# A fixed order for the score matmuls and DFT shares of one cycle

## The chip, the cores and the metric

The kernel runs on one core of one Trainium2 chip. The metric is the device time of the kernel in microseconds (us); three runs of the kernel before gave a median of 2001.87 us (2001.1 to 2004.49).

## The reference

The output is a gated mix of two blocks over x (2048 rows, 640 features, float32):

```python
g = sigmoid((x * gate_w).sum(-1, keepdims=True))
a = mha(x, wqkv, wo)          # 32 heads of 20: softmax(q k^T / sqrt(20)) v, then @ wo
b = dft_seq_re @ (x @ dft_hid_re.T) - dft_seq_im @ (x @ dft_hid_im.T)
return g * a + (1 - g) * b
```

`wqkv` and `wo` are scaled by 64, so scores are large and the softmax needs the true row maximum.

## The kernel before, in words

A first part (the page's slices up to about 280 us) projects q, k and v, stores them to DRAM scratch and starts the hidden DFT. After the loop described next, a last part (from about 1922 us) multiplies by `wo`, gates and stores.

The **main loop** does everything else together. The heads go in pairs; one head of a pair lies on partitions 0 to 63 of `kst` and `qst`, the other on 64 to 127, so that a matmul on one head uses one row half of TensorE. A unit `n` is a head pair and half of the 2048 queries; a unit has 32 steps `i`, and a step has two scores of each of two kinds, one for each head `h`:

- **e** (L636 in `mixed`): keys by queries with the row maximum already in two extra rows of `q`, read by ScalarE's exponential (L639) into a probability tile `p`.
- **m** (L151 in `s_mm`): queries by keys, 41 steps (`LEAD`) ahead, read by VectorE's maximum (L153) into `mx`. It serves only to get the row maxima of a later unit.

Each of the two takes the next of five PSUM banks in turn (`bank()`, `ps`); a bank comes free when its reader has ended. Every score takes its bank in the order in which the program issues it, so each waits for the reader of the score five earlier.

Between the scores stand the **shares** of the DFT (`fill`): each `next(fills)` issues two matmuls of 320 columns, one on each row half, into the two banks `yp` (L287 in the hidden DFT, L509 in the sequence DFT). A hidden tile has 15 shares, a unit of the sequence DFT 48; at the end of either, ScalarE and VectorE read the two banks (L295 and L296, L528 and L529), put on a list by the share and issued at the next burst by `run_extras`. POOL prepares the operands of the sequence DFT.

Every fourth step ends a **cycle** with the **burst**: `av_step` twice, 16 matmuls of the probabilities of the four steps past with the values (L434). They use all 128 rows, four columns' groups at once.

When a unit's maxima are complete, `s_end` negates and joins them (L159, `nms`), and two steps later calls `max_chain`: a transpose on TensorE (L179, it takes a bank too), a cast and a subtract on VectorE (L94 and L95, `m`), and two steps later four small DMAs on SP's queue into the two extra rows of `q`.

The order of work is written out by hand: the program's order is each engine's order. In the kernel before, a step is: e of head 0, m of head 1, shares, e of head 1, m of head 0, shares (in the fourth step of a cycle the burst instead). So a cycle has seven places for shares. `goals` says how many shares are to be done by each place; it deals out 15 for each of the first 54 cycles, and 48 over three or four cycles for each of the 56 units of the sequence DFT. The transpose, where there is one, comes just before the burst, in the cycle's last step.

Of the kernel before, what the change touches and what calls it, by code (L numbers as in the profile page):

```python
# [12 lines left out]
AF = mybir.ActivationFunctionType  # L13
# [5 lines left out]
P = 128  # L19
# [3 lines left out]
DH = 20  # L23
ND = D // P
NS = S // P
NP = H // 2
HE = D // 2
VW = 2 * (DH + 1)
KROWS = 3 * DH
NU = 2 * NP  # L30
BW = HE + 2
LEAD = 41
HEAD = 10

# [16 lines left out]
def f32(ap):  # L51
    return ap.bitcast(F32)
# [3 lines left out]
def mix_kernel(ctx: ExitStack, tc: tile.TileContext, xa, wqk, wb, cdft, wo, out):  # L56
    nc = tc.nc
    pe, act, dve, pool, sp = nc.tensor, nc.scalar, nc.vector, nc.gpsimd, nc.sync
# [23 lines left out]
    kst = [const.tile([P, S], R, name=f"kst{i}") for i in range(2)]  # L82
# [7 lines left out]
    def split(dst1, dst2, src, e1, e2):  # L90
        if e1 is act:
            act.activation(dst1, src, AF.Copy)  # L92
        else:
            e1.tensor_copy(dst1, src)  # L94
        e2.tensor_tensor(dst2, src, f32(dst1), op=ALU.subtract)  # L95
# [8 lines left out]
    def bank():  # L104
        return ps_w.tile([P, 512], F32, name=f"ps{next(turn) % 5}")

    def pair_tile():
        return work.tile([P, 2, 512], F32, name="p", bufs=5)
# [10 lines left out]
    def load_stack(p):  # L119
        kt, qt = kst[p % 2], qst[p % 2]  # L120
        u = S // 2
        for t, o, two, one, cs in ((kt, D, 0, 2, slice(0, S)), (qt, 0, 1, 0, slice(0, u)), (qt, 0, 1, 0, slice(u, S))):
            for h in range(2):
                r = (2 * p + h) * DH
                b = 64 * h
                rows = slice(o + r, o + r + DH)
                yield f32(t[b + two * DH : b + (two + 2) * DH, cs]), qk_scr[:, rows, cs]
                yield f32(t[b + one * DH : b + (one + 1) * DH, cs]), qk_scr[0, rows, cs]

    def q_unit(n):  # L130
        u = n % 2 * (S // 2)
        return qst[n // 2 % 2][:, u : u + S // 2]

    mx, nms = {}, {}
    now, later = [-1], {}

    def at_step(i, fn):
        later.setdefault(i, []).append(fn)


    def s_mm(i, h):
        n, s = divmod(i, 32)
        if n >= NU:
            return lambda: None
        qt, kc = divmod(s, 4)
        q, k = q_unit(n), kst[(n // 2) % 2]
        if n not in mx:
            mx[n] = small.tile([P, 2, 8, 4], F32, name="mx", bufs=2)
        ps = bank()
        b = 64 * h  # L150
        pe.matmul(ps, q[b : b + KROWS, qt * P : (qt + 1) * P],  # L151
                  k[b : b + KROWS, kc * 512 : (kc + 1) * 512], start=True, stop=True)
        return lambda: dve.tensor_reduce(mx[n][:, h, qt, kc : kc + 1], ps, axis=AX.X, op=ALU.max)  # L153

    def s_end(i):
        n, s = divmod(i, 32)
        if n < NU and s == 31:
            nms[n] = small.tile([P, 16], F32, name="nm", bufs=2)
            dve.tensor_reduce(nms[n], mx.pop(n).rearrange("p h q c -> p (h q) c"), axis=AX.X, op=ALU.max, negate=True)  # L159
        if s == 1 and 0 < n <= NU:  # L160
            max_chain(n - 1)

    def s_step(i):
        for fn in [s_mm(i, h) for h in range(2)]:
# [11 lines left out]
    def max_chain(n):  # L176
        q = q_unit(n)
        pt = bank()[:16, :P]
        pe.transpose(pt, nms.pop(n), ident)  # L179
        m1 = small.tile([16, P], R, name="m1", bufs=2)  # L180
        m2 = small.tile([16, P], R, name="m2", bufs=2)
        split(m1, m2, pt, dve, dve)

        def rows():
            for h in range(2):
                b = 64 * h + KROWS
                sp.dma_start(f32(q[b : b + 1, :]), f32(m1[8 * h : 8 * h + 8, :]))
                sp.dma_start(f32(q[b + 1 : b + 2, :]), f32(m2[8 * h : 8 * h + 8, :]))

        if now[0] < 0:  # L190
            rows()
        else:
            at_step(now[0] + 2, rows)
# [27 lines left out]
    def load_wb(j, e1=act, e2=dve):  # L221
        raws = []
        for d in range(0, ND, 3):
            n = min(3, ND - d)
            raw = raw_tile()[:, : n * BW].rearrange("p (d c) -> p d c", d=n)
            sp.dma_start(raw, wb[j, :, d : d + n])
            raws.append((d, n, raw))

        def finish():
            w = proj.tile([P, 2, ND, BW], R, name="wb", bufs=2)  # L230
            for d, n, raw in raws:
# [7 lines left out]
    def flush(keep=0):  # L239
        while len(stores) > keep:  # L240
            sp.dma_start(*stores.pop(0))
# [118 lines left out]
    for n, c in enumerate(order):  # L360
        for t in range(4):
            m = 4 * n + t
# [4 lines left out]
            if t == 1:  # L367
                fin()
                if n + 2 < len(order):
                    fin = load_wqk(order[n + 2])  # L370
    run_s(LEAD)
    flush()
# [16 lines left out]
    cparts, vts, pts = {}, {}, {}  # L389
# [38 lines left out]
    def av_step(i, n, kt):  # L428
        v = vts[n // 2]
        pp = [pts.pop((n, kt, qc)) for qc in range(2)]  # L430
        for qc in range(2):
            for h in range(2):
                j = 2 * qc + h
                pe.matmul(av[32 * j : 32 * j + DH + 1, :], v[:, kt, h * (DH + 1) : (h + 1) * (DH + 1)],  # L434
                          pp[qc][:, h, :], start=kt == 0, stop=kt == NS - 1)
        if kt == NS - 1:
            unit_end(i, n)
# [110 lines left out]
    def run_extras(g, most):  # L548
        while extras and most and extras[0][0] <= now[0]:
            extras.pop(0)[1]()  # L550
            most -= 1
        if more(g):
            n = g // (HT * NS) + 1
            preps.append(load_a(n, made.setdefault(n, 0)))
            made[n] += 1
        if len(preps) > 2 or preps and not more(g):
            preps.pop(0)()
# [8 lines left out]
    def start_dft():  # L566
        flush()
        proj.release()
        apool.append(pools(name="apool", bufs=1))
# [13 lines left out]
    total = 32 * NU  # L583
    done = 0
    goals, fins = {}, {}
# [4 lines left out]
    HID = 4 * NS - HEAD  # L590
# [4 lines left out]
    start = 4 * HID  # L595
    HIDS = HID * 3 * ND
# [4 lines left out]
    cycles += [(edge[u], edge[u + 1], 3 * NS) for u in range(UNITS)]  # L601
    at_goal = 0
    for c0, c1, count in cycles:
        slots = [(4 * c + k, z) for c in range(c0, c1) for k in (1, 2, 3, 4) for z in range(2 - k // 4)]
        for f, slot in enumerate(slots):
            goals[slot] = at_goal + count * (f + 1) // len(slots)
        at_goal += count

    def fill(i, z):
        nonlocal done  # L610
        while done < goals.get((i, z), 0):
            next(fills)
            done += 1

    for i in range(total + 1):
        now[0] = i
        n, s = divmod(i, 32)
        for fn in later.pop(i, ()):
            fn()
        if s % 2 == 0:  # L620
            flush()
        if i < total:
            kt, qc = divmod(s, 2)
            if s == 0 and n % 2 == 0:
                p = n // 2
                if p + 1 < NP:
                    at_step(i + 6, functools.partial(load_v, p + 1))
                    for j, args in enumerate(load_stack(p + 1)):
                        at_step(i + 2 + 2 * j, functools.partial(pool.dma_start, *args))
            q, k = q_unit(n), kst[(n // 2) % 2]  # L630
            pp = pts[n, kt, qc] = pair_tile()

            def mixed(h):
                b = 64 * h
                pt = bank()
                pe.matmul(pt, k[b : b + KROWS + 2, kt * P : (kt + 1) * P],  # L636
                          q[b : b + KROWS + 2, qc * 512 : (qc + 1) * 512], start=True, stop=True)
                most = s_mm(i + LEAD, 1 - h)
                act.activation(pp[:, h], pt, AF.Exp, scale=float(DH) ** -0.5)  # L639
                most()  # L640

            mixed(0)
            fill(i, 0)
            mixed(1)
            s_end(i + LEAD)
        if start + 2 <= i < start + 2 + HT:
            for k in range(2):
                at_step(i + 3, load_a(0, 2 * (i - start - 2) + k))
        if i and i % 4 == 0:
            run_extras(max(done - HIDS, 0) // 3, 2)  # L650
            j = i // 2 - 2
            for kt in (j, j + 1):
                av_step(i, kt // NS, kt % NS)
        else:
            fill(i, 1)
        if i % 4 == 2:
            c = i // 4
            if c + HEAD in (NS, 2 * NS):
                load_wb(3 + (c + HEAD) // NS, pool, pool)()
            if c in (HID - 5, HID - 3):  # L660
                load_c((c - HID + 5) // 2)()
            if c == HID + 1:
                cfin.append(load_c(2))
        if i == start:
            start_dft()
        if total - 10 <= i < total - 4 and i % 2 == 0:
            tt = (i - total + 10) // 2
            fins[tt] = load_o(tt)
        if i == total - 3:
            fins[0]()  # L670
    assert done == at_goal
    now[0] = total + 4
    run_extras(2 * NS * UNITS, 99)
# [76 lines left out]
```

## Time and profile before

| | |
|---|---|
| median of three runs | 2001.87 us (2001.1 to 2004.49) |
| the profiled execution's own time | 2004.27 us |
| its span, first to last instruction | 2002.5 us |
| mean granted TensorE clock | 0.996 |
| busy: TensorE, VectorE, ScalarE, POOL | 99%, 71%, 63%, 55% of the span |
| maxima (L153) | 2048, mean 682 ns |
| exponentials (L639) | 2048, mean 599 ns |
| e and m scores (L636, L151) | 2048 each |
| matmuls of the sequence DFT (L509) | 5376 |
| matmuls of the bursts (L434) | 4096 |

A row of the timeline gives the start in us from the span's start, the length in us, the engine (PE is TensorE's matmul, PEld its weight load, DVE VectorE, ACT ScalarE), the line, the tiles and how many instructions were merged into the row; in brackets stands the idle time before it and what ended it. A row of a group gives the count, the busy time in us, the mean ns of one, and the idle time before them. A matmul's recorded length begins when it is handed to the array, and includes the wait for its weights.

### The profile page before, as it was taken

The page shows a single profiled execution, that of the slowest core. Times are in us where ns is not written, and L with a number is a line of the kernel's source. Part 1 is how long each engine was busy: PE and PEld are TensorE (multiplying, and loading weights), DVE is VectorE, ACT ScalarE, POOL GpSimd, SP SyncE. Part 2 cuts the span into 40 slices and gives each one's busy share as a digit, 9 for nine tenths or more (in the row PEclk, how much of TensorE's full clock was granted, in tenths as well). Part 3 has the DMA queues.
Part 4 walks back from the last instruction along what each step waited for, and adds up shares of the span by engine and source line. Part 5 has one row for each costly group of instructions (what it writes and reads, how often), then busy time and mean ns, then how long its engine had stood idle before and what let it go on. Part 6 is the DMA issues. An engine that isn't in the chain of part 4 may idle for free. (4 is left out here: it accounts for less than half of the span.)

```text
span 2002.5 us, 44148 instructions
## 1 busy us (share of the span) xinstructions
PE 1972.5 (99%) x17080; PEld 1402.0 (70%) x17080; DVE 1428.3 (71%) x2419; ACT 1253.5 (63%) x2337; POOL 1096.9 (55%) x1010
## 2 busy tenths in 40 slices
PE   8999999999999999999999999999999999999998
PEld 7987767666775666666666666666666666666678
DVE  3144568878887788778877877888778877887323
ACT  4221147767776667667766766677667766676741
POOL 1210001111005999657479888994776789777534
PEclk9999999999999999999999999999999999999999
DMA  7654321312115475435266747563545566453355
GB/s 223 166 169 142 126 80 45 83 50 78 40 52 163 148 212 156 119 110 150 88 169 195 204 138 202 187 188 106 158 145 143 155 176 191 143 165 119 99 152 180
DMA packets 196514, 281.05 MB, mean 140 GB/s; under 512 B 73372, under 2 KB 137916, under 8 KB 194384
## 3 DMA queue, kind: packets, MB, share of 16 engines
q1 hardware_dynamic: 158992, 246.20, 40.2%
q0 software_dynamic: 37312, 32.03, 6.5%
q8 instruction: 134, 2.20, 0.5%
q14 instruction: 76, 0.62, 0.1%
HBM read 213.81 MB, written 63.70 MB: 139 GB/s over the span
## 5 line engine op out<-in xcount | busy, mean ns | idle before, releaser
L153 DVE TENSOR_REDUCE mx<-ps 128x1 f32<-128x512 f32 x2048 | 1263.7, 682 | 294.7 <-PE ps L151 281.3
L639 ACT ACTIVATE p<-ps 128x512 f32<-128x512 f32 x2048 | 1122.5, 599 | 438.8 <-PE ps L151 334.5
L151 PE MATMUL ps<-kst,qst 60*128 60x512 f32 x2048 | 924.2, 459 | 9.2 <-ACT p L639 4.1
L636 PE MATMUL ps<-qst,kst 62*128 62x512 f32 x2048 | 818.9, 407 | 2.1 <-DVE mx L153 0.9
L509 PE MATMUL yp<-a,part 64*128 64x320 f32 x5376 | 736.9, 309 | 0.1
L509 PEld LDWEIGHTS yp<-a,part 64*128 64x128 f32 x5376 | 596.8, 187 | 23.5 <-DVE m L529 0.3
L636 PEld LDWEIGHTS ps<-qst,kst 62*128 62x128 f32 x2048 | 378.1, 185 | 222.9 <-issue 74.3
L434 PE MATMUL av<-p,v 128*21 128x512 f32 x4096 | 494.0, 598 | 0.1
L151 PEld LDWEIGHTS ps<-kst,qst 60*128 60x128 f32 x2048 | 372.6, 184 | 61.6 <-ACT p L639 27.4
L95 POOL TENSOR_TENSOR part<-raw,part 128x1024 fp32r<-128x1024 f32 x112 | 267.1, 2385 | 9.0
L434 PEld LDWEIGHTS av<-p,v 128*21 128x21 f32 x4096 | 98.5, 100 | 225.8 <-issue 218.6
L287 PE MATMUL yp<-wb,xs 64*128 64x320 f32 x1920 | 239.9, 311 | 0.0
L287 PEld LDWEIGHTS yp<-wb,xs 64*128 64x128 f32 x1920 | 208.4, 189 | 8.5
L405 POOL TENSOR_TENSOR raw<-raw,raw 128x1024 f32<-128x1024 f32 x78 | 187.6, 2405 | 18.3 <-DMA raw<-in_cdft 13.1
L94 POOL CAST part<-raw 128x1024 fp32r<-128x1024 f32 x112 | 116.2, 1038 | 109.0 <-PE yp L509 104.4
L94 POOL CAST wb<-raw 128x966 fp32r<-128x966 f32 (+1 forms) x4 | 3.4, 858 | 228.6 <-DMA raw<-in_wb 228.6
L466 POOL TENSOR_TENSOR o<-o,rb 128x512 f32<-128x512 f32 x32 | 41.4, 1295 | 153.3 <-DMA rb<-r_scr 117.6
L95 POOL TENSOR_TENSOR a<-araw,a 128x320 fp32r<-128x320 f32 x112 | 97.6, 871 | 9.0
L540 POOL TENSOR_TENSOR yt<-yt,m 128x320 f32<-128x320 f32 x64 | 55.1, 873 | 84.4 <-DVE m L529 82.4
L95 DVE TENSOR_TENSOR p<-ps,p 128x512 fp32r<-128x512 f32 x40 | 27.4, 690 | 94.2 <-ACT p L92 91.4
L98 PE MATMUL ps<-xs,part 128*128 128x512 f32 x200 | 80.3, 401 | 7.4 <-ACT xs L92 6.1
L92 ACT ACTIVATE p<-ps 128x512 fp32r<-128x512 f32 x40 | 23.7, 597 | 101.5 <-PE ps L100 101.5
(68 smaller groups left out, 1386.7 us busy)
## 6 DMA issues: line engine op xcount, KB each, us to landing
raw<-in_cdft SPq DMA_DIRECT2D x192, 512.0 KB
araw<-a_scr SPq DMA_DIRECT2D x192, 160.0 KB
qk_scr<-p SPq DMA_DIRECT2D x40, 512.0 KB
y_scr<-yt SPq DMA_DIRECT2D x96, 160.0 KB
kst<-qk_scr POOLq DMA_DIRECT2D x32, 320.0 KB, 13.1
qst<-qk_scr POOLq DMA_DIRECT2D x64, 160.0 KB, 8.5
a_scr<-raw SPq DMA_DIRECT2D x64, 160.0 KB
yt<-y_scr SPq DMA_DIRECT2D x64, 160.0 KB
```

Source lines behind the costliest of these rows:

```text
L94: e1.tensor_copy(dst1, src)
L95: e2.tensor_tensor(dst2, src, f32(dst1), op=ALU.subtract)
L98: pe.matmul(ps, st1, mv1, start=first, stop=False)
L151: pe.matmul(ps, q[b : b + KROWS, qt * P : (qt + 1) * P], k[b : b + KROWS, kc * 512 : (kc + 1) * 512], start=True, stop=True)
L153: return lambda: dve.tensor_reduce(mx[n][:, h, qt, kc : kc + 1], ps, axis=AX.X, op=ALU.max)
L287: pe.matmul(yp[h][:, :HE], xs[r, xz, d, cs], w[r, wz, d, :HE], start=d == 0 and z == 0, stop=d == ND - 1 and z == 2)
L405: pool.tensor_tensor(raws[0], raws[0], raws[1], op=ALU.add if PRODUCTS[n][0][1][0] > 0 else ALU.subtract)
L434: pe.matmul(av[32 * j : 32 * j + DH + 1, :], v[:, kt, h * (DH + 1) : (h + 1) * (DH + 1)], pp[qc][:, h, :], start=kt == 0, stop=kt == NS - 1)
L509: pe.matmul(yp[h][:, :HE], c[r, cz, cs], a[r, az], start=s == 0 and z == 0, stop=s == NS - 1 and z == 2)
L540: pool.tensor_tensor(y, y, m, op=ALU.add if sg > 0 else ALU.subtract)
L636: pe.matmul(pt, k[b : b + KROWS + 2, kt * P : (kt + 1) * P], q[b : b + KROWS + 2, qc * 512 : (qc + 1) * 512], start=True, stop=True)
L639: act.activation(pp[:, h], pt, AF.Exp, scale=float(DH) ** -0.5)
```

## The change

The two kinds of scores become two streams with a position each, and one string fixes the order of a whole cycle: `e` and `m` are the next score of either kind, `F` a place for shares, `B` the burst. `FIRST` says on which head a step begins, for each of the four steps of a cycle. The places for shares are 15 instead of 7, and each cycle gets its part of a unit's shares. What a step did at its begin and at its end moves into `begin` and `end`, called with its first and second e. Before the first cycle stand `e m m e`. The calls of `max_chain` are put on a list in the loop and made after the burst's matmuls instead of before them.

```diff
+ORDER = "emFemFFFFemFeFFmeFFemFFFmmFFmeeB"
+FIRST = {"e": (0, 0, 1, 1), "m": (1, 1, 1, 1)}
...
         if s == 1 and 0 < n <= NU:
-            max_chain(n - 1)
+            if now[0] < 0:
+                max_chain(n - 1)
+            else:
+                chains.append(n - 1)
...
-        slots = [(4 * c + k, z) for c in range(c0, c1) for k in (1, 2, 3, 4) for z in range(2 - k // 4)]
-        for f, slot in enumerate(slots):
-            goals[slot] = at_goal + count * (f + 1) // len(slots)
-        at_goal += count
+        for c in range(c0, c1):
+            share = count * (c + 1 - c0) // (c1 - c0) - count * (c - c0) // (c1 - c0)
+            places = ORDER.count("F")
+            goals[c] = [at_goal + share * (f + 1) // places for f in range(places)]
+            at_goal += share
...
-            mixed(0)
-            fill(i, 0)
-            mixed(1)
-            s_end(i + LEAD)
...
+    def score(kind):
+        x = heads[kind]
+        heads[kind] += 1
+        i, z = divmod(x, 2)
+        h = z ^ FIRST[kind][(i - (LEAD if kind == "m" else 0) - 1) % 4]
+        if kind == "m":
+            s_mm(i, h)()
+            if z:
+                s_end(i)
+            return
+        if z == 0 and i <= total:
+            begin(i)
+        if i < total:
...
+            pe.matmul(pt, k[b : b + KROWS + 2, kt * P : (kt + 1) * P],
+                      q[b : b + KROWS + 2, qc * 512 : (qc + 1) * 512], start=True, stop=True)
+            act.activation(pts[n, kt, qc][:, h], pt, AF.Exp, scale=float(DH) ** -0.5)
+            if z:
+                end(i)
+
+    def burst(c):
+        run_extras(max(done - HIDS, 0) // 3, 2)
+        for kt in (2 * c, 2 * c + 1):
+            av_step(now[0], kt // NS, kt % NS)
+        while chains:
+            max_chain(chains.pop(0))
+        if c == HID - 1:
+            start_dft()
+
+    for kind in "emme":
+        score(kind)
+    for c in range(total // 4):
+        for kind in ORDER:
+            if kind == "F":
+                fill(c)
+            elif kind == "B":
+                burst(c)
+            else:
+                score(kind)
```

More of the change, by code (lines that the diff above doesn't have):

```diff
@@ L132, in q_unit @@
         return qst[n // 2 % 2][:, u : u + S // 2]
-    mx, nms = {}, {}
+    mx, nms, chains = {}, {}, []
     now, later = [-1], {}
@@ L603, in mix_kernel, with fill, begin @@
     for c0, c1, count in cycles:
-        slots = [(4 * c + k, z) for c in range(c0, c1) for k in (1, 2, 3, 4) for z in range(2 - k // 4)]
-        for f, slot in enumerate(slots):
-            goals[slot] = at_goal + count * (f + 1) // len(slots)
-        at_goal += count
-    def fill(i, z):
+        for c in range(c0, c1):
[3 more added lines that the diff above has]
+            at_goal += share
+    def fill(c):
         nonlocal done
-        while done < goals.get((i, z), 0):
+        goal = goals[c].pop(0) if c in goals else 0
+        while done < goal:
             next(fills)
             done += 1
-    for i in range(total + 1):
+    def begin(i):
         now[0] = i
@@ L621, in mix_kernel, with end @@
             flush()
-        if i < total:
[L623 to L640, printed above, removed]
-            mixed(0)
-            fill(i, 0)
-            mixed(1)
-            s_end(i + LEAD)
+        if s == 0 and n % 2 == 0:
+            p = n // 2
+            if p + 1 < NP:
+                at_step(i + 6, functools.partial(load_v, p + 1))
+                for j, args in enumerate(load_stack(p + 1)):
+                    at_step(i + 2 + 2 * j, functools.partial(pool.dma_start, *args))
+        if i < total:
+            pts[n, s // 2, s % 2] = pair_tile()
+    def end(i):
         if start + 2 <= i < start + 2 + HT:
@@ L648, in mix_kernel @@
                 at_step(i + 3, load_a(0, 2 * (i - start - 2) + k))
[L649 to L655, printed above, removed]
         if i % 4 == 2:
@@ L663, in mix_kernel @@
                 cfin.append(load_c(2))
-        if i == start:
-            start_dft()
         if total - 10 <= i < total - 4 and i % 2 == 0:
@@ L670, in mix_kernel @@
             fins[0]()
+    heads = {"e": 0, "m": 2 * LEAD}
+    def score(kind):
[11 more added lines that the diff above has]
+        if i < total:
+            n, s = divmod(i, 32)
+            kt, qc = divmod(s, 2)
+            q, k = q_unit(n), kst[(n // 2) % 2]
+            b = 64 * h
+            pt = bank()
+            pe.matmul(pt, k[b : b + KROWS + 2, kt * P : (kt + 1) * P],
[21 more added lines that the diff above has]
+                score(kind)
     assert done == at_goal
```

## The prediction

> **What bounds the kernel now.** I read the page first, then the timeline of single engines over one cycle, then the burst-to-burst distances.
>
> ```profile
> span 2002.5 us, 44148 instructions
> PE 1972.5 (99%) x17080; PEld 1402.0 (70%) x17080; DVE 1428.3 (71%) x2419; ACT 1253.5 (63%) x2337; POOL 1096.9 (55%) x1010
> ...
> L153 DVE TENSOR_REDUCE mx<-ps 128x1 f32<-128x512 f32 x2048 | 1263.7, 682 | 294.7 <-PE ps L151 281.3
> L639 ACT ACTIVATE p<-ps 128x512 f32<-128x512 f32 x2048 | 1122.5, 599 | 438.8 <-PE ps L151 334.5
> ```
>
> TensorE looks full, but a matmul counts as busy while it waits for its weights, so 99% doesn't tell whether it streams. VectorE (one maximum over each score tile, L153) and ScalarE (one exponential, L639) each wait some 300 us for scores. So no engine is at its limit all the time: the three hand five PSUM banks round, and each waits in turn. One cycle, from a burst of 16 value matmuls to the next, shows it:
>
> ```profile
> 1208.51 1.92 PE L434 MATMUL av<-p,v 128*21 128x512 f32 x16
> 1210.35 0.49 PE L636 MATMUL ps<-qst,kst 62*128 62x512 f32 x1
> 1210.36 0.50 PE L151 MATMUL ps<-kst,qst 60*128 60x512 f32 x1
> 1210.68 0.32 PE L509 MATMUL yp<-a,part 64*128 64x320 f32 x2
> 1210.84 0.40 PE L151 MATMUL ps<-kst,qst 60*128 60x512 f32 x1
> 1210.84 0.39 PE L636 MATMUL ps<-qst,kst 62*128 62x512 f32 x1
> 1211.07 0.46 PE L509 MATMUL yp<-a,part 64*128 64x320 f32 x4
> 1211.37 0.39 PE L636 MATMUL ps<-qst,kst 62*128 62x512 f32 x1
> 1211.59 0.49 PE L151 MATMUL ps<-kst,qst 60*128 60x512 f32 x1
> 1211.60 0.78 PE L509 MATMUL yp<-a,part 64*128 64x320 f32 x4
> ...
> 1214.47 0.39 PE L151 MATMUL ps<-kst,qst 60*128 60x512 f32 x1
> 1214.79 0.63 PE L434 MATMUL av<-p,v 128*21 128x512 f32 x4
> ```
>
> Call L636 e (its reader is the exponential), L151 m (its reader is the maximum), and a share F two matmuls, one on each row half. Each half runs its own stream: score to next matmul 0.23 (1210.84 to 1211.07), share to next 0.15 (two shares in 0.30, 1211.07 to 1211.37), last score to burst 0.32, burst to next scores 1.84. The prices of a wait and of the readers:
>
> ```profile
> 1210.35 0.18 PEld L636 LDWEIGHTS ps<-qst,kst 62*128 62x128 f32 x1 [0.85 <-DVE mx L153]
> ...
> 1210.46 0.19 PEld L509 LDWEIGHTS yp<-a,part 64*128 64x128 f32 x2
> ...
> 1211.59 0.18 PEld L151 LDWEIGHTS ps<-kst,qst 60*128 60x128 f32 x1 [0.18 <-ACT p L639]
> ```
>
> ```profile
> 1208.14 1.09 ACT L639 ACTIVATE p<-ps 128x512 f32<-128x512 f32 x2 [0.20 <-PE ps L636]
> 1210.94 3.29 ACT L639 ACTIVATE p<-ps 128x512 f32<-128x512 f32 x6 [1.72 <-PE ps L151]
> ```
>
> ```profile
> 1210.92 4.88 DVE L153 TENSOR_REDUCE mx<-ps 128x1 f32<-128x512 f32 x8 [1.37 <-PE ps L151]
> ```
>
> A weight load that couldn't be made ahead puts 0.105 in front of its matmul (1210.35 to 1210.46). Exponentials follow each other at 0.49 (1.09 less 0.60), maxima at 0.60 (4.88 less 0.68, over 7). A reader starts 0.10 (ACT) or 0.06 (DVE) after the recorded end of its matmul, which lies 0.39 after the true start. The m at 1211.59 needs the bank of the exponential that began at 1210.94 and took 0.60: the hand-over costs 0.05. ACT idles 1.72 and DVE 1.37 around the burst, because only the maximum and exponential begun just before it are left to read.
>
> **What the waits cost.** On one half a cycle holds 8 scores, n shares and the burst's edges: 8 x 0.23 + 0.15 n + (0.09 + 1.84 + 0.105) = 3.88 + 0.15 n. The loop has 54 cycles with n = 15, then 198 with 56 x 48 shares, which the code deals out as 78 cycles of 16 and 120 of 12; the last 11 have no m left, so 76 and 112 with m.
>
> ```profile
> 318.47 1.91 PE L434 MATMUL av<-p,v 128*21 128x512 f32 x16
> ...
> 324.94 0.63 PE L434 MATMUL av<-p,v 128*21 128x512 f32 x4
> ```
>
> ```profile
> 1343.50 1.91 PE L434 MATMUL av<-p,v 128*21 128x512 f32 x16
> ...
> 1350.08 1.91 PE L434 MATMUL av<-p,v 128*21 128x512 f32 x16
> ...
> 1356.67 0.28 PE L179 MATMUL ps<-ident,nm 128*16 128x128 f32 x1
> 1356.88 1.91 PE L434 MATMUL av<-p,v 128*21 128x512 f32 x16
> ```
>
> Taken: 6.28 (n = 12, 1208.51 to 1214.79), 6.47 (15), 6.58 (16), against sums of 5.68, 6.13 and 6.28. So waits cost 0.60, 0.34 and 0.30 a cycle, some 110 us in all: no new order can bring more than this.
>
> **The new order, walked through.** It keeps every matmul, reader and share; only the sequence differs. I walk one cycle with n = 12, in us from its first score, by one rule: a score starts at the latest of its half's previous matmul plus 0.23 or 0.15, and its bank's reader start plus 0.60 (ACT) or 0.68 (DVE) plus 0.05 plus 0.105. The bank is that of five scores before. Start / reader start:
> e 0.00/0.49, m 0.00/0.45, e 0.23/0.98, m 0.23/1.05; three F; e 1.06/1.55; m 1.25 (bank of the first exp)/1.70; e 1.48/2.04; two F; m 1.74 (third score's exp)/2.30; e 2.01/2.53; two F; e 2.31 (bank of the exp at 1.55)/3.02; m 2.54 (max at 1.70)/2.99; two F; m 2.84/3.59; m 3.13 (max at 2.30)/4.19; two F; m 3.44/4.79; e 3.78 (exp at 3.02)/4.27; e 3.82 (max at 2.99)/4.76. The burst starts at 4.14, the next cycle at 4.14 + 1.95 = 6.09. The same walk gives 6.30 for n = 15 and 6.31 to 6.38 for 16, where it leaves hardly a wait. Applied to the old order it gives 6.35, 6.50 and 6.65, which is 0.03 to 0.07 above the trace; that is its error. What it shows: three maxima now stand in line when the burst begins (3.59, 4.19, 4.79), so DVE reads until 1.3 us behind its start (4.79 + 0.68 - 4.14) instead of 1.0 (1210.92 less 1.37, less 1208.51), and two or three shares stand wherever the next bank isn't back yet.
>
> Gain against the trace: 112 x 0.19 + 53 x 0.17 + 76 x 0.25 = 21 + 9 + 19 = 49 us. The 11 cycles without m are bounded by their sum in both orders: nothing.
>
> **The moved transposes.** Once in 8 cycles (30 times) the transpose L179, with a cast and a subtract on DVE, moves from ahead of the burst to behind it.
>
> ```profile
> 1357.56 0.27 DVE L94 CAST m<-ps 16x128 fp32r<-16x128 f32 x1
> 1357.86 0.28 DVE L95 TENSOR_TENSOR m<-ps,m 16x128 fp32r<-16x128 f32 x1
> ```
>
> Before, such a cycle takes 6.80 (1350.08 to 1356.88) instead of 6.58: it costs 0.22, 0.21 of it TensorE's. Behind the burst TensorE's 0.21 stays; the 0.55 on DVE, which lay in the burst's idle time, now can stand ahead of the first maximum, and the transposed bank shifts the round by one. No row shows a transpose behind a burst. Bounds: below, 0 if it fits into the 1.84's drain (it can't gain more, since its matmul remains); above, 0.21 + 0.55 = 0.76. I take 0.35, as the walk with the split put first gives, nearer to the row of 0.21: 30 x (0.35 - 0.22) = +4 us, bounds -7 to +16. Its four DMA issues keep their step, two steps on, and their place on SP's queue; the split that they wait for ends 1.84 + 0.28 + 0.06 + 0.57 = 2.75 behind the burst's start instead of 1.26 (1358.14 less 1356.88), so what SP holds behind them goes 1.5 us later. The rows are needed six steps, some 9 us, after: I cost that at nothing, and if a row came late its unit would wait, at most the 1.5, 30 x 1.5 = 45 us. POOL's issues keep their steps.
>
> **The DFT banks' readers.** At the end of a tile both banks are read behind the last scores' readers:
>
> ```profile
> L529 DVE TENSOR_TENSOR m<-yp,m 128x320 f32<-128x320 f32 x56 | 27.4, 488 | 43.4 <-ACT m L528 41.7
> ...
> L528 ACT ACTIVATE m<-yp 128x320 f32<-128x320 f32 x56 | 24.9, 444 | 0.0
> ```
>
> ACT gets there at 4.76 + 0.49 - 4.14 = 1.11 behind the burst's start, DVE at 1.60, and the banks are back at 2.14, while the next tile's first share could load at 1.95 and start at 2.18. So it starts at 2.14 + 0.105, 0.06 late. For the 53 tiles of the cycles of 15 that is in the 6.30; the 56 others add 3 us.
>
> Sum: -49 + 4 + 3 = -42 from the profiled execution's 2004.27, hence 1962; that execution lies 2.4 above the median of the three (2001.87), so 1960.
>
> **One stream or two.** That each half runs on by itself carries the walk, and has a row:
>
> ```profile
> 1211.60 0.56 PE L509 MATMUL yp<-a,part 64*128 64x320 f32 x2
> ```
>
> It is the timeline's answer for the stretch 1211.84 to 1211.87: a second share matmul runs already, while the m of 1211.59 (true start 1211.70) holds its half to 1211.93. So it is the first half's second share, and it started ahead of the other half's first, which precedes it in the program. If the order held over both halves, a share behind a lone score would wait 0.08 (0.23 - 0.15) for the other half; cycles of 12 and 15 have waits that cover this, those of 16 have none: 76 x 0.08 = 6 us, so 1966. The Trainium skill ("TensorE: Matmul & The Clock Gate", Part 3, "The mechanism") states that order: matmuls start and end strictly as the program has them. This trace disagrees with it.
>
> **Rivals.**
> - POOL sets the pace.
>
> ```profile
> 700.00:750.00 50.00, 49.94 (x465) 34.31 (x467) 40.83 (x70) 35.52 (x66) 48.47 (x48) 1.00 0.71 207
> ...
> 1300.00:1350.00 50.00, 50.00 (x469) 34.98 (x465) 40.29 (x69) 35.66 (x66) 48.30 (x46) 1.00 0.67 188
> ```
>
> In such stretches POOL, which prepares the DFT's operands, is busy 97% (fifth engine column), and a cycle 3% shorter would ask it for 100%. Against it: those are a few hundred us, and elsewhere it is at half to four fifths. If half the gain of the DFT's cycles (40) goes: 1980.
> - Waits only change place: if DVE is the true limiter, sums stay near 2000. Against: 1.37 idle each cycle.
> - One order over both halves, as above: 1966.
> - Slower: a score without a partner blocks both halves. The old order always issues e and m on opposite halves together; the new one leaves one e before two F and the last e before the burst alone. If TensorE can't overlap a lone score with a share of the other half, each adds up to 0.23, 0.46 a cycle: 241 x 0.46 - 42 = +69, 2071. It decides from 0.09 per lone score on (42 / 482). For it: no row shows a lone score; against it: the row above, where share and score of different halves overlap.
>
> **Chances.** Forecast 0.71 (1946 to 1974: the walk's error, 0.03 to 0.07 a cycle, is 241 x 0.05 = 12 us either way), POOL 0.13 (to 1986), one order 0.03, waits moved 0.03, lone scores 0.10. About 0.2% (4 us) can be told from no change. Faster 0.87, same 0.03, slower 0.10. The range 1946 to 1986 leaves out the last two cases and a little on either side.
>
> **What would show it.** Burst to burst 6.09, 6.30 and about 6.33 for 12, 15 and 16 shares; DVE reading some 1.3 us into each burst, and its waits on L151 falling from 281 us; about 0.35 more where L179 stands behind a burst. Cycles at or above the old 6.28 to 6.58 would refute the walk; lone scores with both halves still behind them would show the slow rival; POOL at 100% with TensorE waiting on part or a, the first.

## The result, and the profile after

The changed kernel takes 1972.9 us (median of four runs, 1972.1 to 1976.8) against 2001.99: ratio 0.986, 95% interval 0.985 to 0.987. That is 29 us faster, where 42 were forecast. The page of the changed kernel, span, engines and the two readers (maximum now L161, exponential L684):

```profile
span 1970.6 us, 43800 instructions
PE 1928.0 (98%) x17080; PEld 1384.3 (70%) x17080; DVE 1454.8 (74%) x2419; ACT 1212.2 (62%) x2337; POOL 1097.4 (56%) x1010
...
L161 DVE TENSOR_REDUCE mx<-ps 128x1 f32<-128x512 f32 x2048 | 1288.3, 684 | 210.4 <-PE ps L159 191.8
L684 ACT ACTIVATE p<-ps 128x512 f32<-128x512 f32 x2048 | 1081.0, 599 | 451.8 <-PE ps L159 244.4
```

VectorE waits 192 us for its scores (L159 is m, L682 e, L520 a share, L445 the burst) instead of 281; ScalarE's idle time before its exponentials stays near 450 (438.8 before, 451.8 now). The timeline of TensorE over one cycle of 12 shares:

```profile
1260.04 1.92 PE L445 MATMUL av<-p,v 128*21 128x512 f32 x16
1261.89 0.49 PE L682 MATMUL ps<-qst,kst 62*128 62x512 f32 x1
1261.89 0.72 PE L159 MATMUL ps<-kst,qst 60*128 60x512 f32 x2
...
1263.04 0.39 PE L682 MATMUL ps<-qst,kst 62*128 62x512 f32 x1
1263.13 0.49 PE L159 MATMUL ps<-kst,qst 60*128 60x512 f32 x1
1263.27 0.48 PE L520 MATMUL yp<-a,part 64*128 64x320 f32 x2
1263.47 0.39 PE L682 MATMUL ps<-qst,kst 62*128 62x512 f32 x1
...
1265.40 0.39 PE L159 MATMUL ps<-kst,qst 60*128 60x512 f32 x1
1265.49 0.31 PE L520 MATMUL yp<-a,part 64*128 64x320 f32 x1
1265.64 0.55 PE L682 MATMUL ps<-qst,kst 62*128 62x512 f32 x2
1266.12 0.63 PE L445 MATMUL av<-p,v 128*21 128x512 f32 x4
```

and of VectorE around the same burst:

```profile
1259.47 1.88 DVE L161 TENSOR_REDUCE mx<-ps 128x1 f32<-128x512 f32 x3
1262.45 4.38 DVE L161 TENSOR_REDUCE mx<-ps 128x1 f32<-128x512 f32 x7 [1.10 <-PE ps L159]
```

Count from the first score's true start (1261.89 + 0.105). The walk put the third pair's e at 1.06, its m at 1.25, the lone e at 1.48, the last m at 3.44 and the burst at 4.14; the trace has 1.05, 1.24, 1.48, 3.41 and 4.13. VectorE reads until 1261.35, 1.31 behind the burst's start, where 1.3 was forecast. The cycle takes 6.08. For 16 and 15 shares the bursts' rows say:

```profile
1371.89 1.92 PE L445 MATMUL av<-p,v 128*21 128x512 f32 x16
1378.19 0.63 PE L445 MATMUL av<-p,v 128*21 128x512 f32 x4
```

```profile
330.66 1.91 PE L445 MATMUL av<-p,v 128*21 128x512 f32 x16
336.90 1.92 PE L445 MATMUL av<-p,v 128*21 128x512 f32 x16
```

6.30 and 6.24. Burst to burst, the medians of all cycles that have no transpose in them or next to them are 6.10, 6.31 and 6.24 (12, 16 and 15 shares) instead of 6.29, 6.59 and 6.47. At that rate 112, 76 and 53 cycles save 21 + 21 + 12 = 54 us. But from the first burst to the last the loop shortened only from 1640.9 to 1608.6, by 32. Some 20 us were lost in single long cycles: twelve of more than 6.95 us lie 29 us above the medians, where the old kernel has four that lie 10 above. The longest in the sequence DFT's part lasted 11.02 us (TensorE, then ScalarE, then POOL):

```profile
743.93 0.49 PE L682 MATMUL ps<-qst,kst 62*128 62x512 f32 x1
...
745.24 0.39 PE L682 MATMUL ps<-qst,kst 62*128 62x512 f32 x1
748.37 0.50 PE L159 MATMUL ps<-kst,qst 60*128 60x512 f32 x1 [2.75 <-ACT p L684]
...
750.10 0.63 PE L159 MATMUL ps<-kst,qst 60*128 60x512 f32 x1
```

```profile
747.23 0.60 ACT L452 ACTIVATE o<-av 128x512 f32<-128x512 f32 x1 [4.07 <-DMA o_scr<-o]
747.72 3.25 ACT L684 ACTIVATE p<-ps 128x512 f32<-128x512 f32 x6
```

```profile
737.16 2.44 POOL L416 TENSOR_TENSOR raw<-raw,raw 128x1024 f32<-128x1024 f32 x1
739.67 1.05 POOL L102 CAST part<-raw 128x1024 fp32r<-128x1024 f32 x1
740.80 2.36 POOL L103 TENSOR_TENSOR part<-raw,part 128x1024 fp32r<-128x1024 f32 x1
743.12 1.28 POOL L477 TENSOR_TENSOR o<-o,rb 128x512 f32<-128x512 f32 x1
```

Read from the bottom: POOL, with hardly a gap since 692, prepares the DFT's operands in program order, so it normalises the last unit's `o` (L477) only at 743.12. Its store to `o_scr` follows, and there is one buffer for `o`: ScalarE's copy of the next unit (L452) waits 4.07 us for the store. The exponentials stand behind that copy, the scores wait for their banks, TensorE stands still, and at 750.10 a score takes 0.63 instead of 0.39 because the granted clock has dropped. A second place is the first m of a new head pair, which needs `qst`. The waits of TensorE on it, whole span:

```profile
PE ps L159 <- DMA qst<-qk_scr: 4.6, 3, 2.3
```

### The profile page after: what moved, and what is told of

Same layout as the page of the kernel before. It is cut to its first block, busy times and chain, and to the rows that moved or that the text cites. A ratio compares the mean times of both kernels' runs of the same rounds, so it can differ in the third digit from the quotient of the medians.

```text
span 1970.6 us, 43800 instructions
## 1 busy us (share of the span) xinstructions
PE 1928.0 (98%) x17080; PEld 1384.3 (70%) x17080; DVE 1454.8 (74%) x2419; ACT 1212.2 (62%) x2337; POOL 1097.4 (56%) x1010
## 5 line engine op out<-in xcount | busy, mean ns | idle before, releaser
L161 DVE TENSOR_REDUCE mx<-ps 128x1 f32<-128x512 f32 x2048 | 1288.3, 684 | 210.4 <-PE ps L159 191.8
L684 ACT ACTIVATE p<-ps 128x512 f32<-128x512 f32 x2048 | 1081.0, 599 | 451.8 <-PE ps L159 244.4
L159 PE MATMUL ps<-kst,qst 60*128 60x512 f32 x2048 | 778.3, 428 | 19.6 <-ACT p L684 8.9
L682 PE MATMUL ps<-qst,kst 62*128 62x512 f32 x2048 | 705.2, 424 | 3.7 <-DMA qst<-m 2.2
L520 PE MATMUL yp<-a,part 64*128 64x320 f32 x5376 | 689.9, 310 | 0.1
L520 PEld LDWEIGHTS yp<-a,part 64*128 64x128 f32 x5376 | 595.2, 187 | 15.5 <-DVE m L540 0.3
L445 PE MATMUL av<-p,v 128*21 128x512 f32 x4096 | 493.3, 597 | 0.1
L682 PEld LDWEIGHTS ps<-qst,kst 62*128 62x128 f32 x2048 | 339.1, 185 | 212.6 <-DVE mx L161 179.3
L159 PEld LDWEIGHTS ps<-kst,qst 60*128 60x128 f32 x2048 | 366.0, 185 | 51.2 <-ACT p L684 12.3
L445 PEld LDWEIGHTS av<-p,v 128*21 128x21 f32 x4096 | 98.2, 100 | 226.3 <-issue 222.7
L102 POOL CAST part<-raw 128x1024 fp32r<-128x1024 f32 x112 | 116.3, 1039 | 18.3 <-PE yp L520 12.5
L477 POOL TENSOR_TENSOR o<-o,rb 128x512 f32<-128x512 f32 x32 | 41.5, 1296 | 133.7 <-DMA rb<-r_scr 131.5
```

The costliest lines, as they stand in the source:

```text
L159: pe.matmul(ps, q[b : b + KROWS, qt * P : (qt + 1) * P], k[b : b + KROWS, kc * 512 : (kc + 1) * 512], start=True, stop=True)
L520: pe.matmul(yp[h][:, :HE], c[r, cz, cs], a[r, az], start=s == 0 and z == 0, stop=s == NS - 1 and z == 2)
L682: pe.matmul(pt, k[b : b + KROWS + 2, kt * P : (kt + 1) * P], q[b : b + KROWS + 2, qc * 512 : (qc + 1) * 512], start=True, stop=True)
L684: act.activation(pts[n, kt, qc][:, h], pt, AF.Exp, scale=float(DH) ** -0.5)
```

## The experiments

**Which part of the order carries the gain.** Pairs as before, with finer shares and the moved transposes kept:

```diff
-ORDER = "emFemFFFFemFeFFmeFFemFFFmmFFmeeB"
-FIRST = {"e": (0, 0, 1, 1), "m": (1, 1, 1, 1)}
+ORDER = "emFemFFFFemFFemFFemFemFFFemFFemB"
+FIRST = {"e": (0, 0, 0, 0), "m": (1, 1, 1, 1)}
```

> The changed kernel with e and m always paired on opposite halves and no run of maxima at the burst, but 15 places for the shares and the transposes behind the burst kept. Theory A (the maxima standing in line at the burst carry the gain): the hand walk gives 6.31, 6.43 and 6.58 us a cycle for 12, 15 and 16 shares, the old kernel's, so about 2000 us. Rival B (the finer spread of the shares carries it): the cycles stay at 6.10, 6.24 and 6.31, so 1973.

2006.01 us, ratio 1.0025 (1.001 to 1.004). The timeline of this kernel's bursts, then of its VectorE:

```profile
1264.63 1.91 PE L445 MATMUL av<-p,v 128*21 128x512 f32 x16
1270.93 0.63 PE L445 MATMUL av<-p,v 128*21 128x512 f32 x4
```

```profile
1264.43 1.27 DVE L161 TENSOR_REDUCE mx<-ps 128x1 f32<-128x512 f32 x2
1267.04 4.30 DVE L161 TENSOR_REDUCE mx<-ps 128x1 f32<-128x512 f32 x7 [1.34 <-PE ps L159]
```

6.30 for 12 shares, and 6.45 and 6.58 as medians for 15 and 16: the old cycle, with VectorE idle 1.34 again. The finer spread by itself brings nothing.

**The other reader at the burst.** The letters exchanged, also in the four scores that stand before the first cycle:

```diff
+ORDER = "meFmeFFFFmeFmFFemFFmeFFFeeFFemmB"
+FIRST = {"e": (1, 1, 1, 1), "m": (0, 0, 1, 1)}
```

> The changed kernel with the letters e and m exchanged in the fixed order, so that three exponentials instead of three maxima stand in line when the burst begins. Theory A: VectorE, the slower reader (0.60 against 0.49), is left idle at the burst and its eight maxima must be read between bursts: the walk gives 6.57 to 6.58 a cycle, about 2045 to 2065 us, slower than before. Rival (any grouping of one reader's scores at the burst will do): about 1973.

2047.11 us, ratio 1.023 (1.021 to 1.025): slower than before, as theory A said. The medians are 6.55 to 6.57 whatever the number of shares, so TensorE's own work no longer shows; with 3 exponentials in line at the burst the slower reader is the one left idle, 331 us before its maxima where the changed kernel has 210. The page's row of this kernel:

```profile
L161 DVE TENSOR_REDUCE mx<-ps 128x1 f32<-128x512 f32 x2048 | 1275.4, 682 | 330.7 <-PE ps L682 168.9
```

**Where the shares stand.** Scores as in the change, shares dealt evenly:

```diff
+ORDER = "emFFemFFemFFeFFmeFFemFFFmmFFmeeB"
```

> The changed kernel with its sequence of scores kept and its 15 places for the shares dealt out evenly (two behind each pair early in the cycle, not four behind the second). Theory A: half the gain is the sequence, half is that shares stand where the next bank is not back: the walk gives 6.25, 6.40 and 6.46, about 1995 us. Rival B (only the fine spread matters): 1973 or less.

2000.5 us, ratio 0.9998 (0.9985 to 1.001). The medians are 6.24, 6.39 and 6.45 (walk: 6.25, 6.40, 6.46), which is worth some 21 of the 54 us; single long cycles took most of that back. So the change needs both: maxima in line at the burst, and shares held back from the start of the cycle, where banks are free, for the places where they aren't.

**The transposes.** Ahead of the burst again, in the new order:

```diff
     def burst(c):
         run_extras(max(done - HIDS, 0) // 3, 2)
+        while chains:
+            max_chain(chains.pop(0))
         for kt in (2 * c, 2 * c + 1):
             av_step(now[0], kt // NS, kt % NS)
-        while chains:
-            max_chain(chains.pop(0))
```

> The changed kernel with the transposes of the maxima ahead of the burst's matmuls again, 30 in the loop. If the move costs what the two traces show (0.33 a transpose behind, 0.22 ahead): 3 us faster than the changed kernel, 1970. Rival: the move is itself a gain, then 1975 or more. Rival: the moved transposes are why the gain fell short, then 1960.

1978.65 us, ratio 0.989 (0.987 to 0.991); the interval touches the changed kernel's. Behind the burst in the old order (the calls put on a list as in the change):

```diff
             for kt in (j, j + 1):
                 av_step(i, kt // NS, kt % NS)
+            while chains:
+                max_chain(chains.pop(0))
```

> The old kernel with its 30 transposes moved behind the burst and nothing else changed: the prediction's own term for them. By that term a transpose costs 0.35 a cycle behind the burst instead of 0.22 ahead: 4 us slower than before, 2006. Rival: it is free behind the burst, where VectorE idles anyway: 1996 (30 times 0.22 less). Rival F (the move only pays when three maxima stand in line, as the changed kernel with the transposes ahead, 1979, suggests): 2002 to 2006 here.

2001.4 us, ratio 0.9984 (0.9973 to 0.9994). So my cost for the move had the wrong sign. In the new order the move is a gain of about 6 us. In the old order it is a small one at most: 1 to 5 us by the interval, though the medians of these runs (2001.87 and 2001.4) are only 0.5 apart. For the new order, the weight load of the transpose in the kernel with the transposes ahead shows why:

```profile
1290.44 0.27 PEld L682 LDWEIGHTS ps<-qst,kst 62*128 62x128 f32 x2
1291.13 0.09 PEld L190 LDWEIGHTS ps<-ident,nm 128*16 128x16 f32 x1 [0.41 <-DVE mx L161]
1291.33 0.14 PEld L445 LDWEIGHTS av<-p,v 128*21 128x21 f32 x8
```

A transpose takes a bank, and ahead of the burst that bank still has to be read: it waits 0.41 for a maximum, and the burst behind it waits too. Behind the burst all banks but the last few have been read. Per transpose, the cycle that ends with its burst and the next together cost 0.44 to 0.53 more than the medians ahead of the burst in the new order, and 0.27 to 0.36 behind it. In the old order they cost 0.17 to 0.27 ahead and 0.15 to 0.21 behind; no run shows where that small gain comes from.

**Where the missing 20 us went.** Two buffers for `o`:

```diff
-        o = pa.tile([P, 512], F32, name="o")
+        o = pa.tile([P, 512], F32, name="o", bufs=2)
```

> The changed kernel with two buffers for the tile o, so that ScalarE's copy out of the value banks at a unit's end need not wait for the store of the unit before. Theory C (the lost 20 us are single stalls in which POOL's backlog holds up the normalisation of o, its store, and through the one buffer ScalarE): the cycles of 11.37, 11.02 and 9.74 us and the two half-clock windows behind two of them go, about 1960. Rival D (the operands of the DFT themselves come late): those cycles stay long, about 1972.

1957.09 us, ratio 0.978 (0.976 to 0.979). ScalarE's waits before L452, first in the changed kernel, then with two buffers:

```profile
ACT o L452 <- DMA o_scr<-o: 12.5, 4, 4.2
```

```profile
ACT o L452 <- PE av L445: 20.4, 28, 1.1
ACT o L452 <- issue: 2.3, 4, 0.6
```

Four waits for the store, 12.5 us, are gone, and the three cycles of 11.37, 11.02 and 9.74 with them. The old kernel has one such wait, and the same edit was made there:

```profile
ACT o L441 <- DMA o_scr<-o: 4.1, 1, 4.1
```

> The old kernel with two buffers for o. It has one stall of that kind (the cycle of 10.84 us at 429): 4 to 6 us less, 1997. If the two buffers were a gain of their own, whatever the order: 16 us less as in the changed kernel, 1986.

1998.56 us, ratio 0.998 (0.997 to 0.999): 3 us, for the one stall that was there (10.84 us at 429; its counterpart in the changed kernel is the cycle of 11.37 at 425). So the buffer is worth 16 us behind the faster order and 3 behind the old one. The difference, 13 us, is gain of the new order that was given back through `o`.

Then POOL's load itself: the additions that combine two operands of the DFT, in two places, left out of both kernels (their DFT is incomplete, so they serve for timing only):

```diff
-                pool.tensor_tensor(raws[0], raws[0], raws[1], op=...)
+                pass
```

> The changed kernel without the 158 additions on POOL (188 and 70 us) that combine two DFT operands into one; the DFT's result is left wrong by it. Theory C and rival D both: without POOL's backlog the stalls behind cycle 57 go, 15 to 18 us, 1955 to 1960. Rival E (the stalls come from the faster score order itself): 1973 stays.

> The old kernel with the same additions on POOL left out. Its trace has some 3 us of stalls behind cycle 57 and 5 where the sequence DFT begins, so 1994 to 2000; less the light changed kernel, the order alone is then worth 40 to 45 us. Rival E: the gap stays at 29.

1950.52 us and 1999.17 us (ratios 0.975, 0.973 to 0.977, and 0.998, 0.997 to 0.999). Engines of the light changed and the light old kernel:

```profile
PE 1921.2 (99%) x17080; PEld 1380.4 (71%) x17080; DVE 1453.0 (75%) x2419; ACT 1211.5 (62%) x2337; POOL 835.0 (43%) x850
```

```profile
PE 1968.9 (99%) x17080; PEld 1399.6 (70%) x17080; DVE 1427.8 (72%) x2419; ACT 1253.0 (63%) x2337; POOL 835.3 (42%) x850
```

With POOL at 43% the order is worth 1999.2 - 1950.5 = 49 us. POOL's 262 us were worth 3 to the old order and 22 to the new one. TensorE's waits for `qst<-qk_scr` are gone in both light kernels.

**What is left of POOL's backlog.** The pair's loads from another queue, on top of two buffers:

```diff
-                    at_step(i + 2 + 2 * j, functools.partial(pool.dma_start, *args))
+                    at_step(i + 2 + 2 * j, functools.partial(sp.dma_start, *args))
```

> The changed kernel with two buffers for o, and the 12 loads of each head pair's kst and qst issued from SP's queue instead of from POOL's, where they stand behind POOL's operands. Theory C: the long cycles in which a pair's first maxima wait for qst (7.34, 7.99, 6.97, 7.62 us) go as well, 4 to 6 us under the kernel with two buffers alone, about 1955. Rival: SP's queue holds them up as long, behind its own waits for POOL, VectorE and ScalarE, and nothing is won or the time is longer.

2070.0 us, ratio 1.033 (1.031 to 1.035). The rival held, and more than I allowed for. SP's waits between 660 and 1980 us, longest first:

```profile
SPq L632 <- DMA kst<-qk_scr: 107.9, 25, 8.4
SPq L461 <- ACT o L452: 85.4, 20, 7.5
SPq L632 <- POOL yt L551: 81.3, 24, 9.3
```

The loads wait there behind stores that wait for POOL all the same, and TensorE waits up to 10.5 us for `qst`. The loads every step instead of every second one, from POOL's queue again and with two buffers:

```diff
-                    at_step(i + 2 + 2 * j, functools.partial(pool.dma_start, *args))
+                    at_step(i + 2 + j, functools.partial(pool.dma_start, *args))
```

> The changed kernel with two buffers for o and the 12 loads of a head pair issued every step instead of every second one, still from POOL's queue. Theory C (POOL's backlog lets qst land behind the first maxima that need it): the long cycles of a pair's first maxima (7.13, 8.25, 7.76, 8.72 us in the kernel with two buffers) fall to about 6.25, 7 to 8 us less, 1949. Rival: the loads then wait on POOL's queue for the pair before and stop POOL, no gain or slower than 1957.

1960.38 us, ratio 0.978 (0.976 to 0.980), the same as with two buffers alone. The waits for `qst<-qk_scr` are gone, but POOL now stops for its own loads:

```profile
1115.07 1.16 POOL L632 DMA_DIRECT2D qst<-qk_scr  x2 [4.14 <-DMA kst<-qk_scr]
```

and within the next 30 us a share waits 1.6 us for its operand; in the whole span TensorE now waits 5.9 us for row maxima (`qst<-m`), where two buffers alone had 0.5. Two buffers for `o`, at 1957, is the fastest complete kernel here.

The waits for `qst` are not a price of the faster order alone. The kernel with pairs has the old cycle, and as many waits for the store of `o` as the old kernel (one, of 4.3 us), but it waits three times for `qst`, 7.2 us in all, where the old kernel waits once:

```profile
PE ps L151 <- DMA qst<-qk_scr: 2.0, 1, 2.0
```

Which part of the rewritten loop brings them, no run separates.

No run was aimed at the stalls where the sequence DFT begins (one cycle of 11.47 us at 614 in the changed kernel, 9.77 at 622 in the old, 13.59 at 607 with two buffers). The light kernels bear on them all the same: there that cycle takes 6.35 and 6.67, so these stalls go with POOL's additions too. By which wait is open.

## Why the prediction was right and wrong

The sign, the range (1946 to 1986) and the mechanism held; the size was 29 us where 42 was the sum. Step by step:

- **The walk** was right to 0.03 us in every position compared and to 0.06 in the three cycles (6.09, 6.30, 6.33 against 6.10, 6.24, 6.31). Its term of 49 us measured 54 in the undisturbed cycles, and the two light kernels, transposes included, are 49 apart. Redone by its own rule, the listing has two slips that change nothing behind them: four shares, not three, stand behind the second pair (the times and the trace have four), and the last m comes out at 3.37, not 3.44.
- **Two streams on the two halves** held. The lone e at 1263.47 starts when its own half is done with the m (1.24 + 0.23 = 1.47), while the other half has been running matmuls of the next two shares since 1263.27, although these stand behind the e in the program. The rival of lone scores that block both halves is out: it needed 0.09 for each.
- **One order over both halves** is out too: it gave 6.39 for the cycles of 16 shares.
- **The banks' readers** at a tile's end: 6.24 for the cycles of 15 shares, each with such an end, leaves no room for the delay of 0.06. It was part of the walk's 6.30; without it the same rule gives 6.24.
- **The transposes**: +4 us was forecast, and the kernel as a whole shows some +3 (0.27 to 0.36 behind the burst against 0.17 to 0.27 before). But that the size came out is luck, because the reasoning was wrong: the new order makes them dearer wherever they stand, and the move makes them cheaper in it. I had priced the move without asking whether the bank that a transpose needs is free. (The loop's traces hold 31 transposes, not 30.)
- **The step that failed** is the sum's silence on POOL. I had it as a rival in which POOL sets the pace of half the DFT's cycles (1980, chance 0.13). The forecast itself took POOL's backlog at nothing: I set against the rival only that the stretches with POOL at 97% are a few hundred us long, and looked for its sign only in TensorE's waits for `part` or `a`. What happened lies between: the pace stayed TensorE's, and POOL's lateness came through two side doors, the store of `o` that ScalarE's copy waits for (12.5 us of waits against 4.1, and 13 us of the gain), and the loads of `qst` that stand in POOL's queue (4.6 us against 2.0, and not tied to the pace). The old profile had both already, as one wait each; I hadn't asked what else stands in POOL's program order.

## What to carry to other kernels

Where two readers of different speed drain the same banks, try letting the slower one's tiles stand in line when a stretch without new tiles begins, and keep filler work for the places where the next bank isn't back. Here a cycle's schedule could be worked out by hand from some ten durations, read off the rows of one cycle. Before a loop gets faster, list everything that stands in program order on the engine that is nearly full in places, not only its main product: a small step queued there (a store, a load's issue) may hold the single buffer on which the fast path depends. Here a second buffer there cost one argument and brought 16 us, where the change itself had brought 29.

## What the runs showed of the hardware

A pause of TensorE can cost more than its length. The stretch before and the stretch from 749.70 of the changed kernel (the columns are PE, PEld, DVE, ACT and POOL busy, then the granted clock):

```profile
742.10:749.70 7.60, 4.86 (x46) 2.91 (x47) 2.21 (x5) 3.53 (x7) 7.45 (x7) 1.00 0.45 126
749.70:753.10 3.40, 3.40 (x22) 2.92 (x19) 2.81 (x5) 1.27 (x3) 3.26 (x3) 0.50 0.60 228
```

After the gap of 2.75 us the clock is granted at half for 3.4 us; by an estimate, half of that, some 1.7 us, is lost in addition. All four pauses of TensorE of 2 us or more in this kernel's loop (3.21, 2.28, 2.75 and 2.02 us, ending at 432, 623, 748 and 1155) are followed by such a stretch, and its longest other pauses, of 1.42, by none. One more stretch, at 644, stands behind no such pause.

The Trainium skill ("TensorE: Matmul & The Clock Gate", Part 1) describes a gate that falls to half after an idle window of about 3.4 us and comes back after a busy one. The length of the half-speed stretch agrees with it; but the pauses that came before it here, 2.02 to 3.21 us, are all shorter than that window.
